# New order of the first steps, and biases through TensorE, in a windowed attention with a softplus feed-forward behind it

## The chip, the cores and the metric

The kernel runs on one core of a Trainium2 chip. A core has five engines with instruction streams of their own: TensorE (PE, matrix products into PSUM), VectorE (DVE), ScalarE (ACT, functions such as exp and ln), GpSimd (POOL) and SyncE (SP). Each works through its own instructions in the order in which the program gives them, and waits on semaphores for the others. In this kernel POOL issues the loads that cast from float32 to bfloat16, and SP issues the transposes by DMA and the stores. The metric is the time of one execution on the device in microseconds (us).

## The reference

Four sequences of 768 tokens, 8 heads of 64; 3072 tokens in all. The attention sees the first 8 tokens of the sequence and the last 96 tokens; each head has a penalty that is linear in the distance. What comes out goes through a feed-forward layer of width 2048 with softplus.

```
scores = (q @ k.T) / 8                               # per batch and head
rel = pos[:, None] - pos[None, :]
keep = (pos[None, :] < 8) | ((rel >= 0) & (rel < 96))
dist = where(is_global & ~is_local, 96, abs(rel))
scores = where(keep, scores - slope[h] * dist, -1e9) # slope[h] = 2 ** -(h + 1)
a = softmax(scores)
x = (a @ v) laid out as (3072, 512)
g = softplus(x @ w_in)                               # w_in 512 x 2048
out = g @ w_out                                      # w_out 2048 x 512
```

## The kernel before, in words

The tokens are cut into 24 blocks of 128, six to a sequence, and the feed-forward works on 12 chunks of 256 tokens, two blocks to a chunk. All steps have short names, and the order in which they stand in the program is the order on every engine.

For block n:

- `lN` loads q and k of block N, `lvN` loads v (L97, on POOL, 128 KB each in bfloat16). Block 0's q and k come in float32 over SP (L84, L85) and are cast on VectorE (`cq0`, `ck0`, L441 and L444).
- `tN` transposes q and k on TensorE against the identity (L203) and VectorE copies the result to QT and KT (L209, L215). `tq` and `tk` do the same for q and k apart. From block 8 on, `dN` does it by DMA from SP (L227, L228).
- `gkN` and `gvN` copy the keys and values of the sequence's first 8 tokens into the block before (L240, L244), so that the window and the global tokens come out of two blocks.
- `sN.h` makes the scores of half h of the heads: 8 products (4 in a sequence's first block) into `s_ps` (L253), and VectorE adds the bias of the distance into Z (L265 or L267). Each half's scores use the one buffer `s_ps`. From block 8 on both halves are made in one step, the second in the banks `tr` and `o2` (L275, L276).
- `eN.h` takes exp of Z on ScalarE into Pb (L289).
- `pN.h` multiplies Pb with v (L302, in `x_ps`), and VectorE divides by the sum (L313, L316).
- `xN` transposes the result into XT, on TensorE for the first six blocks (L331), by DMA from SP after that (L327).

For the feed-forward, chunk c has 8 steps `f` (number 8c + u): each makes 256 of the 2048 columns with 8 products of 256 columns (L347), and ScalarE makes softplus as ln(1 + exp) from it in two passes (L352, L353). The products go to `hT`, which has two buffers. 8 steps `o` (number 8c + u) multiply the result with w_out in 4 products of 512 columns (L367). `wiN` and `woN` load a quarter each of w_in and w_out (L102, L108, 512 KB each in bfloat16). `gN` is a POOL instruction that waits for step fN, and so holds back POOL's later loads (L404).

The bias tables come from a ramp (POOL, L142) and a few VectorE steps (`tables`), and from 24 ScalarE multiplications: `b0`, `b1` (L181), `bb0`, `bb1` (L185). `wN` is a run of N filler products of 512 columns on zeros (L438), which compute nothing that is used.

The order of the first steps is written out by hand as a text (ORDER, L411 to L422), up to f27. All later steps are sorted by due times: `fN` at N + 0.5, `oN` at N + LAG + 0.9 with LAG = 13, attention of block n around 4n - 10.4 (`steady`, L424).

Of the kernel before, what the change touches and what calls it, by code (L numbers as in the profile page):

```python
# [9 lines left out]
AF = mybir.ActivationFunctionType  # L10
# [9 lines left out]
def kernel(  # L20
# [47 lines left out]

# [10 lines left out]
    w_in_c = [const.tile([P, KM, FW], BF16, name=f"w_in{c}") for c in range(NWC)]  # L79
# [5 lines left out]
    nc.sync.dma_start(k_f[:], k[0, :, 0:P, :].rearrange("h s d -> s h d"))  # L85
# [5 lines left out]
    warm_in = const.tile([P, DM], BF16, name="warm_in")  # L91
# [9 lines left out]
    def load_w_in(c):  # L101
        nc.gpsimd.dma_start(  # L102
            w_in_c[c][:],
            moe_w_in[:, c * FW : (c + 1) * FW].rearrange("(m p) f -> p m f", p=P),
        )
# [40 lines left out]
    make_identity(nc, ident)  # L146
    load_qk(1)
    load_v(0)
    load_v(1)
    load_qk(2)  # L150
    load_qk(3)

    def tables():
        nc.vector.tensor_scalar(
            far_a[:], rampf[:], float(NL - 1), FAR, op0=ALU.is_gt, op1=ALU.mult
        )
# [3 lines left out]
        nc.vector.tensor_copy(dist_0[:], dist_d[:])  # L160
        nc.vector.tensor_scalar_min(dist_0[0:NG, :], dist_0[0:NG, :], float(NL))
        nc.vector.tensor_scalar(
            far_b[:], rampf[:], -float(P - NL + 1), FAR, op0=ALU.is_gt, op1=ALU.mult
        )
        nc.vector.scalar_tensor_tensor(dist_p[:], rampf[:], float(P), far_b[:], ALU.add, ALU.add)
        nc.vector.memset(dist_p[0:NG, :], float(NL))

    tables()
    ones(2, RV)

    load_w_in(0)
    load_v(2)
    load_w_in(1)
    load_v(3)

    def head_of(half, r):
        return 4 * half + 2 * ((r // 2) % 2) + r // 4

    def bias_first(half):
        for r in range(0, 8, 2):  # L180
            nc.scalar.mul(bias0[:, half, r // 2, :], dist_0[:], -slopes[head_of(half, r)])  # L181
# [223 lines left out]


    LAG = 13

    ORDER = """  # L411
# [109 lines left out]
```

## Time and profile before

| what | value |
|---|---|
| time, median of 3 runs | 217.99 us (217.25 to 218.74) |
| profiled execution, first to last instruction | 215.9 us |
| what lies around that span, against the median | 2.1 us |
| TensorE busy | 208.5 us (97%) |
| ScalarE busy | 163.4 us (76%) |
| VectorE busy | 115.8 us (54%) |
| POOL busy | 74.1 us (34%) |

The profiled execution gives the span alone; the 2.1 us is the difference to the median of the runs. Busy TensorE counts every product, fillers too, and a product's row lasts until its last result is written, so that rows overlap; the chain of waits gives the distance at which they follow each other. In the chain and in the timeline the first number is the start in us from the first instruction, the second the length in us. In the group rows, "x768 | 98.5, 273" says 768 instructions, 98.5 us busy, 273 ns each. In a timeline row, square brackets hold the idle time ahead of it and what ended it. "DMA to landing" is the time from the start of the issuing instruction until the data is there. A row of stretches gives the stretch, and then the busy time (and number of instructions) of PE, PEld (weight loads), DVE, ACT and POOL, the granted clock, the DMA share and GB/s.

### The profile page before, as it was taken

How to read it: one execution, taken by the hardware profiler on the slowest of the kernel's cores; microseconds unless marked ns; L12 is line 12 of the kernel's file. 1: busy time of each engine (PE TensorE's matmuls, PEld its weight loads, DVE VectorE, ACT ScalarE, POOL GpSimd, SP SyncE). 2: the span in 40 equal slices, each digit the busy share in tenths (PEclk: the TensorE clock that was granted, in tenths of full speed). 3: DMA queues.
4: the chain of work that ended last, by engine and by line, in shares of the span. 5: the costliest groups of instructions: out<-in, count | busy, mean ns of one | idle time of the engine just before them, and what ended most of it. 6: DMA issues, size and time to landing. Idle time of an engine off the chain costs nothing.

```text
span 215.9 us, 5010 instructions
## 1 busy us (share of the span) xinstructions
PE 208.5 (97%) x1986; PEld 140.8 (65%) x1986; DVE 115.8 (54%) x258; ACT 163.4 (76%) x266; POOL 74.1 (34%) x117
## 2 busy tenths in 40 slices
PE   7789999999999999999999999999999999999994
PEld 2356876666768666666676666667667667666553
DVE  5798933687593464464674674364574573011121
ACT  7746999849898979768878878868978978777300
POOL 8995445524253524334334334343311000000000
PEclk9999999999999999999999999999999999999999
DMA  8999999999998999999999999999992620211112
GB/s 125 152 185 183 207 183 198 164 173 145 140 130 102 146 173 147 142 147 104 155 108 128 153 115 127 154 128 110 161 140 47 98 73 8 68 52 49 49 49 97
DMA packets 109927, 27.06 MB, mean 125 GB/s; under 512 B 102608, under 2 KB 106960, under 8 KB 109904
## 3 DMA queue, kind: packets, MB, share of 16 engines
q0 software_dynamic: 77024, 13.37, 83.2%
q1 hardware_dynamic: 32880, 13.38, 31.3%
q8 instruction: 15, 0.25, 0.5%
q14 instruction: 8, 0.07, 0.1%
HBM read 27.26 MB, written 6.29 MB: 155 GB/s over the span
## 4 chain that ended last, share of the span: by engine, by line
PE 86%; ACT 6%; DVE 4%; DMA 2%; issue 1%; SPq 0%; DVEq 0%
PE o L367 38%; PE hT L347 36%; PE x_ps L302 4%; PE s_ps L253 4%; DVE Z L267 2%; ACT G L353 2%; DMA k_f<-in_k_dram 2%; ACT Pb L289 2%; ACT e_sb L352 2%; PE o L389 2%; PE s_lo L253 1%; PE tr L203 1%; DVE Z L265 1%; DVE k_t L444 0%; PE tr L331 0%
## 5 line engine op out<-in xcount | busy, mean ns | idle before, releaser
L347 PE MATMUL hT<-XT,w_in 128*128 128x256 bf16 x768 | 98.5, 273 | 0.1
L367 PE MATMUL o<-w_out,G 128*128 128x512 bf16 x368 | 92.8, 379 | 0.0
L347 PEld LDWEIGHTS <-w_in 128*128 128x128 bf16 x768 | 74.2, 98 | 25.0 <-issue 0.3
L352 ACT ACTIVATE e_sb<-hT 128x512 f32<-128x512 f32 x96 | 56.5, 588 | 21.8 <-PE hT L347 20.8
L353 ACT ACTIVATE G<-e_sb 128x512 bf16<-128x512 f32 x96 | 60.5, 630 | 3.6
L289 ACT ACTIVATE Pb<-Z 128x1024 bf16<-128x1024 f32 (+1 forms) x48 | 46.7, 977 | 11.1 <-DVE Z L267 9.8
L367 PEld LDWEIGHTS <-G 128*128 128x128 bf16 x368 | 32.2, 98 | 26.9
L267 DVE TENSOR_TENSOR Z<-s_ps,biasA 128x1024 f32<-128x1024 f32 x26 | 31.8, 1222 | 12.3 <-PE s_ps L253 12.3
L313 DVE RECIPROCAL rcp<-x_ps 128x4 f32<-128x4 f32 x48 | 8.7, 181 | 45.7 <-PE x_ps L302 45.5
L373 DVE COPY osb<-o 128x512 f32<-128x512 f32 x23 | 15.8, 685 | 26.6 <-PE o L367 26.5
L404 POOL COPY gate_t<-G 1x1 bf16<-1x1 bf16 x32 | 5.7, 178 | 67.4 <-ACT G L353 67.4
L97 POOL DMA_DIRECT2D q_t<-in_q_dram x23 | 20.5, 892 | 10.6 <-issue 5.3
L97 POOL DMA_DIRECT2D v_t<-in_v_dram x24 | 21.3, 886 | 6.4 <-PE x_ps L302 2.4
L97 POOL DMA_DIRECT2D k_t<-in_k_dram x23 | 20.5, 891 | 4.3 <-PE s_ps L253 1.9
L316 DVE TENSOR_TENSOR xsf<-x_ps,rcp 128x256 bf16<-128x256 f32 x48 | 20.4, 424 | 1.7
L302 PE MATMUL x_ps<-v_t,Pb 128*128 128x65 bf16 x352 | 18.6, 193 | 0.1
L302 PEld LDWEIGHTS <-Pb 128*128 128x128 bf16 x352 | 16.7, 98 | 2.8 <-ACT Pb L289 0.8
L253 PEld LDWEIGHTS <-KT 64*128 64x128 bf16 x352 | 10.3, 94 | 8.4 <-issue 7.0
L253 PE MATMUL s_ps<-QT,KT 64*128 64x128 bf16 x232 | 12.1, 218 | 0.9 <-DVE Z L267 0.6
L438 PE MATMUL warm_ps<-warm_in 128*128 128x512 bf16 x26 | 8.9, 445 | 1.2 <-DVE v_t L89 1.2
L284 DVE TENSOR_TENSOR Z<-s_hi,biasA 128x512 f32<-128x512 f32 x14 | 9.5, 681 | 0.0
L284 DVE TENSOR_TENSOR Z<-s_lo,biasA 128x512 f32<-128x512 f32 x14 | 9.5, 681 | 0.0
(49 smaller groups left out, 81.7 us busy)
## 6 DMA issues: line engine op xcount, KB each, us to landing
out_dram<-osb SPq DMA_DIRECT2D x23, 256.0 KB, 3.2
v_t<-in_v_dram POOLq DMA_DIRECT2D x24, 128.0 KB, 4.6
q_t<-in_q_dram POOLq DMA_DIRECT2D x23, 128.0 KB, 4.6
k_t<-in_k_dram POOLq DMA_DIRECT2D x23, 128.0 KB, 5.1
w_in<-in_moe_w_in_dram POOLq DMA_DIRECT2D x4, 512.0 KB, 9.0
w_out<-in_moe_w_out_dram POOLq DMA_DIRECT2D x4, 512.0 KB, 13.5
XT<-xsf SPq DMA_TRANSPOSE x18, 4.2
q_f<-in_q_dram SPq DMA_DIRECT2D x1, 256.0 KB, 3.3
```

Source lines behind the costliest of these rows:

```text
L97: nc.gpsimd.dma_start(dst[n][:, :, 0:D], src[b, :, i * P : (i + 1) * P, :].rearrange("h s d -> s h d"))
L253: nc.tensor.matmul(dst(4 * sub + 2 * mm + t), KT[n - t][rows, m, :], QT[n][rows, m, :])
L267: nc.vector.tensor_tensor(Z[:], s_ps[:], biasA[:, half, :, :], ALU.add)
L284: nc.vector.tensor_tensor(Z[:, regs, :], s_i[:, 0:4:step, :], bias[:, 1, regs, :], ALU.add)
L289: nc.scalar.activation(Pb[:, 0:nreg, :], Zt.pop((n, half))[:, 0:nreg, :], AF.Exp, scale=inv_sqrt)
L302: nc.tensor.matmul(x_ps[:, lh, :], Pb[:, r, :], v_t[n - t][:, h, :], start=(t == 0), stop=(t == 1 or first),)
L316: nc.vector.tensor_tensor(xsf[:, h0 : h0 + 4, :], x_ps[:, :, 0:D], rcp[:, h0 : h0 + 4][:, :, None].to_broadcast([P, 4, D]), ALU.mult,)
L347: nc.tensor.matmul(hT[:, j, :], w_in_c[wc][:, m, fo : fo + P], XT[c][:, m, :], start=(m == 0), stop=(m == KM - 1),)
L352: nc.scalar.activation(e_sb[:], hT[:], AF.Exp)
L353: nc.scalar.activation(G[c][:, 2 * u : 2 * u + 2, :], e_sb[:], AF.Ln, bias=1.0)
L367: nc.tensor.matmul(o[:], G[c][:, 4 * kq + a, ns * P : ns * P + P], w_out_c[kq][:, a, :], start=(kq == 0 and a == 0), stop=(kq == NWC - 1 a ...
L373: nc.vector.tensor_copy(osb[:], O.pop((c, ns))[:])
```

## The change

Four things change together.

1. **Order.** ORDER is written anew and reaches to f36 and o24 (about token 1400). Loads of q and k become steps of their own (`lq`, `lk`) and all loads stand in ORDER: q, k, v of blocks 1 to 3 come ahead of the first quarter of w_in except for v3. The feed-forward begins with f0 f1 f2, then takes chunk 1's f8 to f11 ahead of chunk 0's f3 to f7, and the weights come in that order. LAG becomes 11. The transposes `x` by DMA are called `y`.
2. **Bias by TensorE.** For blocks 0 to 3 a new step `zN.h` writes minus slope times distance into PSUM by 4 products of a scaled identity (`slope_id`) with the distance table (128 columns in block 0, 256 otherwise), and the scores are added onto it in PSUM. ScalarE takes exp from PSUM. VectorE's additions for these blocks go. The two halves have buffers of their own: `s_ps`, and `oo` in the two banks that are `o` and `o2` later.
3. **Tables.** The distance tables become bfloat16, VectorE makes the identity and the 8 scaled identities, and half 1's bias tables (`b1`, `bb1`) are one ScalarE multiplication each of half 0's.
4. **Small things.** k of block 0 is loaded over ScalarE's DMA queue; fillers have 256 columns, are 16 at the start and then one ahead of single steps, and are written into the buffer of the step behind them; `tk0` uses the bank `tr` as `tq0` does; Pb has four buffers; blocks 0 and 1 use `hT` buffers for half 1 of `p` and for `x`.

```diff
-    nc.sync.dma_start(k_f[:], k[0, :, 0:P, :].rearrange("h s d -> s h d"))
+    nc.scalar.dma_start(k_f[:], k[0, :, 0:P, :].rearrange("h s d -> s h d"))
...
-    make_identity(nc, ident)
-    load_qk(1)
-    load_v(0)
-    load_v(1)
-    load_qk(2)
-    load_qk(3)
...
+    nc.vector.tensor_scalar(ident[:], rampf[:], 0.0, 1.0, op0=ALU.is_equal, op1=ALU.mult)
...
+    for h in range(H):
+        nc.vector.tensor_scalar_mul(slope_id[:, h, :], ident[:], -slopes[h])
...
-    load_w_in(0)
-    load_v(2)
-    load_w_in(1)
-    load_v(3)
...
     def bias_rest(half):
+        if half:
+            nc.scalar.mul(biasA[:, 1, :, :], biasA[:, 0, :, :], HALF_RATIO)
+            return
...
+    def fill(dst):
+        for _ in range(fillers[0]):
+            nc.tensor.matmul(dst, warm_in[:, 0:P], warm_in[:, 0 : dst.shape[1]])
+        fillers[0] = 0
...
-    def qk(n, half, dst):
+    def qk(n, half, dst, pre=False):
...
+                        start=not pre,
+                        stop=not pre or (mm == 1 and (t == 1 or n == first_of(n))),
...
+    NPB = 4
+    def early(n, half):
+        return (oo if half else s_ps)[:, :, :]
+    def z(n, half):
+        buf = early(n, half)
+        fill(wide(buf))
+        for j in range(4):
+            sub, mm = divmod(j, 2)
+            h = 4 * half + 2 * mm + sub
+            if n == first_of(n):
+                nc.tensor.matmul(
+                    buf[:, 2 * j, :], slope_id[:, h, :], dist_0[:], start=j % 2 == 0, stop=False
+                )
+            else:
+                nc.tensor.matmul(
+                    buf[:, 2 * j : 2 * j + 2, :], slope_id[:, h, :], dist_dp[:],
+                    start=j % 2 == 0, stop=False,
+                )
...
     def sc(n, half):
+        if n < NPB:
+            fillers[0] = 0
+            buf = early(n, half)
+            qk(n, half, lambda r: buf[:, r, :], pre=True)
+            return
+        fill(wide(s_ps[:]))
...
     def ex(n, half):
         nreg = 4 if n == first_of(n) else 8
-        Pb = work.tile([P, 8, P], BF16, tag="Pb", name="Pb")
...
+        Pb = work4.tile([P, 8, P], BF16, tag="Pb", name="Pb")
+        if n < NPB:
+            src = early(n, half)[:, 0 : 8 : 8 // nreg, :]
...
-    LAG = 13
+    LAG = 11
     ORDER = """
-        w8 b0 bb1 cq0 ck0 tq0 w1 tk0 w2 s0.0 b1 tq1 bb0 tk1 w1 e0.0 s0.1 e0.1
-        l4 wi2 wi3 wo0 l5 lv4 wo1 lv5 wo2 wo3
-        w2 p0.0 s1.0 t2 l6 lv6 p0.1 e1.0 w1 s1.1 gk2 e1.1 w2 x0 p1.0 w2 s2.0 t3 l7 lv7 e2.0 p1.1
-        w2 s2.1 e2.1 gk3 w2 x1 gv2 w3 s3.0
-        f0 p2.0 f1 s3.1 e3.0 p2.1 e3.1 f2 gv3 t4 gk4 f3 p3.0 x2 s4.0 p3.1 f4 f5 s4.1 x3 f6 gk5
...
+        w16 b0 cq0 ck0 z0.0 tq0 z0.1 b1 tk0 s0.0 bb0 lq1 s0.1 e0.0 lk1 lv0 e0.1 t1 lq2 z1.0 lk2 lv1 z1.1
+        p0.0 p0.1 s1.0 s1.1 e1.0 t2 gk2 x0 p1.0 lq3 w1 z2.0 e1.1 w1 s2.0 lv2 lk3 p1.1 z2.1 wi0 s2.1 e2.0
+        e2.1 gk3 gv2 t3 p2.0 w1 z3.0 x1 lv3 s3.0 p2.1 bb1 e3.0 z3.1 s3.1 e3.1 gv3 x2 p3.0 wi2 f0 lq4 lk4
+        p3.1 f1 x3 f2 lk5 f8 t4 lq5 f9 wo0 wi4 f10 gk4 s4.0 t5 f11 lv4 s4.1 lq6 o4 lk6 o0 wi6 e4.0 gk5 lv5
+        e4.1 f3 gv4 f12 wo1 s5.0 f4 p4.0 t6 f13 s5.1 e5.0 f5 p4.1 lq7 lk7 wo2 f14 lv6 gv5 g9 lq8 lk8 s6.0
+        e5.1 p5.0 x4 f15 s6.1 f6 e6.0 o1 t7 p5.1 wo3 f7 s7.0 g13 lv7 d8 x5 e6.1 lk9 w1 o5 o6 g15 o2 f16 lv8
+        f17 p6.0 s7.1 f18 f19 p6.1 lq9 w1 o7 e7.0 e7.1 f20 g17 y6 d9 w1 gk8 o3 f21 p7.0 s8.0 g19 o8 lq10
...
     def tr_first_k(n):
-        tr = ps.tile([P, 2, NPAIR, P], BF16, tag="o2", name="tr_k")
+        tr = qk_bank()
```

More of the change, by code (lines that the diff above doesn't have):

```diff
@@ L296, in pv @@
         Pb = Pt.pop((n, half))
+        x_b = x_ps
+        if n < 2 and half:
+            x_b = ps2.tile([P, 4, D + 1], F32, tag="hT", name="x_b")
+        fill(wide(x_b[:]))
         for lh in range(4):
@@ L355, in o_bank @@
     def o_bank(i):
[L356 removed]
+        return o_tile(i, [P, DM])
     def ffn2(c, u):
@@ L429, in steady @@
             f"e{n}.0": s + 0.7, f"e{n}.1": s + 1.7, f"p{n}.0": s + 1.95, f"p{n}.1": s + 2.95,
[L430 removed]
+            f"y{n}": s + 3.25,
         }
[L433 removed]
+    fillers = [0]
     def warm(count):
[L437 to L438 removed]
+        fillers[0] += count
     def cast_q(n):
```

144 lines of the change are left out of this document (87 added, 57 removed).

## The prediction

> **What bounds the kernel now.** I read the page first, then the stretches, the timeline of TensorE, and last the chain of waits in order of time.
>
> ```profile
> span 215.9 us, 5010 instructions
> PE 208.5 (97%) x1986; PEld 140.8 (65%) x1986; DVE 115.8 (54%) x258; ACT 163.4 (76%) x266; POOL 74.1 (34%) x117
> ...
> PEclk9999999999999999999999999999999999999999
> ...
> PE 86%; ACT 6%; DVE 4%; DMA 2%; issue 1%; SPq 0%; DVEq 0%
> ```
> ```profile
> 10.00:15.00 5.00, 4.13 (x56) 2.55 (x55) 4.93 (x12) 2.34 (x3) 5.00 (x7) 1.00 1.70 175
> 15.00:20.00 5.00, 4.49 (x53) 2.84 (x54) 4.96 (x10) 2.32 (x3) 2.69 (x4) 1.00 1.83 181
> ...
> 100.00:120.00 20.00, 20.00 (x207) 13.74 (x205) 12.22 (x26) 16.23 (x26) 7.02 (x12) 1.00 1.32 119
> ```
> ```profile
> 1.19 3.32 PE L438 MATMUL warm_ps<-warm_in 128*128 128x512 bf16 x8 [1.19 <-DVE v_t L89]
> ...
> 18.72 1.03 PE L347 MATMUL hT<-XT,w_in 128*128 128x256 bf16 x8
> ...
> 47.78 1.91 PE L347 MATMUL hT<-XT,w_in 128*128 128x256 bf16 x16
> ```
>
> The span lies 2.1 us under the median of 217.99; I take these 2.1 us as fixed. TensorE has no gap in the later stretches (20.00 of 20), so there the time is its work. That can't shrink, since every step stays. Between 10 and 20 us VectorE is full instead (4.93 and 4.96 of 5.00), and part of TensorE's busy time there is filler. The first feed-forward step is at 18.72. So a gain can only come from the start: how early TensorE is full of real work.
>
> The chain of waits gives the spacing of each kind of step, and what carries the start:
>
> ```profile
> 1.26 4.37 DMA k_f<-in_k_dram
> ...
> 5.66 0.71 DVE k_t L444
> ...
> 6.42 0.41 PE tr_k L203 x4
> ...
> 6.85 0.44 DVE KT L215
> ...
> 7.74 0.70 DVE Z L265
> ...
> 10.27 1.23 DVE Z L267
> 11.50 0.02 issue
> 11.52 1.07 ACT Pb L289
> ...
> 23.05 1.04 ACT Pb L289
> 24.09 0.49 ACT e_sb L352
> ...
> 24.60 0.63 ACT G L353
> ...
> 31.40 0.45 PE tr L203 x8
> 31.84 0.86 PE o L367 x4
> 32.71 0.87 PE hT L347 x8
> ...
> 34.44 0.33 PE s_ps L253 x8
> ...
> 37.49 0.24 PE x_ps L302 x8
> ...
> 41.02 0.22 PE tr L331 x4
> ```
>
> From 7.7 to 18.7 the chain is a ring over one buffer: scores, VectorE's addition (0.70 or 1.23), exp (1.07). Now I count **lost time**: the clock minus real TensorE work at these spacings. At 47.78, where f16 begins, done are t0 to t7 (8 x 0.45 = 3.6), scores of blocks 0 to 6 (10 halves x 0.33, and 4 half-sized ones of 0.2: 4.1), p up to p6.0 (10 x 0.24 and 3 x 0.13: 2.8), x0 to x5 (6 x 0.22 = 1.3), 16 f (13.9) and 8 o (6.9): 32.6 us. Lost: 15.2.
>
> **The change, part by part.** *Bias by TensorE.* VectorE loses 2 x 0.70 and 6 x 1.23 = 8.8 us, all of it in the ring. TensorE gains 8 z steps: two of 4 x 128 columns, six of 4 x 256. A z of 1024 columns is half of an f (2048 columns, 0.87): 0.43; together 6 x 0.43 + 2 x 0.22 = 3.0 us. They stand where the fillers stood: 26 fillers of 512 columns become 18 of 256 (16 at the start, one each ahead of z2.0 and z3.0; the others are set to nothing by the step behind them). With that cover gone z would cost its 3.0 us in full. A z waits until exp has read its buffer, and on TensorE behind it stand t, x and p steps; but with two buffers one half's z and scores run beside the other's exp. exp reads PSUM where it read SBUF; the nearest rows are the two passes of a step f, of which the one out of PSUM is not slower (0.49 against 0.63), so nothing; the other end is the difference, 0.14 for each of 8.
>
> *Tables.* The 8 scaled identities are VectorE steps of a kind that the trace lacks:
>
> ```profile
> L154 DVE TENSOR_SCALAR far_a<-rampf 128x128 f32<-128x128 f32 x1 | 0.2, 227 | 0.0
> L160 DVE COPY dist<-dist_d 128x128 f32<-128x128 f32 x1 | 0.5, 457 | 0.0
> L89 DVE MEMSET v_t<- 128x8 bf16 x8 | 0.3, 65 | 0.0
> L185 ACT ACTIVATE biasA<-dist_d 128x128 f32<-128x128 f32 x8 | 2.3, 292 | 0.0
> ```
>
> Between 65 ns and 457 ns each, 0.5 to 3.7 us; I take 0.15, the distance at which L154 and its like follow each other (nearest in kind and size): 1.2 us. The tables ended at 3.8; with the identity they end near 4.9. The cast of q began at 4.07, so it comes 0.8 later, which is hidden, as k lands only at 1.26 + 4.37 = 5.63. At 3.7 us the chain would start 2 us later. On ScalarE, 12 multiplications and two wide ones (bounded by 0.49 and 1.07) replace 24; they end by 6, before the first exp. `bb1` stands ahead of e3.0 and takes 1.0 us there.
>
> *First scores.* k over ScalarE's queue: issuing costs ScalarE about 0.5 ahead of its table load, hidden. Landing between 4.04 (where q landed) and 5.63; I take 5.4. Then 0.71 (cast), 0.44 (copy of QT, now ahead, since `tk0` waits for the bank `tr`), 0.41, 0.44: first scores at 7.45, against 7.33. The Trainium skill, "DMA: Bandwidth & Descriptors", section "Issuing engines are not separate DMA queues", says that another issuing engine saves only the time of issuing. By that k would land at 5.6 and the scores come at 7.65; no run here shows k on ScalarE's queue yet. The next stage absorbs such differences, as follows.
>
> *Blocks 0 to 3.* Exp of a half takes 0.95 to 1.07; e0 at 7.8 to 8.9, s1 at 9.7, e1 to 12.05, e2.1 to 14.4, `bb1`, e3.0 15.4 to 16.4, p3.0, x2, and f0 at 16.85. ScalarE is the ring's limit now, VectorE is not: its copies (0.44 each) fit between.
>
> *Loads.* POOL's issues and landings:
>
> ```profile
> 1.29 0.33 POOL masks.py:199 TENSOR_SCALAR_AFFINE_SELECT ident<-ident 128x128 bf16<-128x128 bf16 x1
> 1.57 1.02 POOL L97 DMA_DIRECT2D q_t<-in_q_dram  x1
> ...
> 7.80 0.93 POOL L97 DMA_DIRECT2D k_t<-in_k_dram  x1
> 8.67 0.81 POOL L102 DMA_DIRECT2D w_in<-in_moe_w_in_dram  x1
> ...
> 13.65 1.60 POOL L102 DMA_DIRECT2D w_in<-in_moe_w_in_dram  x2
> ...
> 30.14 0.89 POOL L97 DMA_DIRECT2D q_t<-in_q_dram  x1 [2.98 <-DMA q_t<-in_q_dram]
> ```
> ```profile
> DMA to landing us min/median/max: 4.6/4.6/4.6
> ```
> ```profile
> DMA to landing us min/median/max: 6.2/6.2/6.2
> ```
> ```profile
> DMA to landing us min/median/max: 9.9/10.8/11.7
> ```
>
> These answers are for k3 (issued 7.80), the first quarter of w_in (8.67) and the next two late ones (13.65, 14.4). They land at 12.4, 14.87, 23.55 and 26.1: 2.5 us per quarter once the queue is full. Between them the q, k, v take 0.85 to 0.9 each, as they are issued. Without the identity POOL starts 0.5 sooner, but v2 now stands ahead too: k3 lands at 12.8, `wi0` at 15.3, `wi2` 18.7, k4 20.4, `wo0` 24.7, `wi4` 27.2, k6 29.9, `wi6` 32.4, `wo1` 35.8, k7 37.6, `wo2` 40.1, `wo3` 45.3.
>
> *From f0 to f16.* I follow the new order, each step at the latest of three: TensorE free, its data landed, its `hT` given back by the exp of the f two before. A step f costs ScalarE 1.14 (0.49 + 0.63 and the way), an exp 0.95 to 1.04. f2 comes at 19.1 (behind wi2), t4 20.85, o4 25.1, f12 27.75, t6 30.05, f14 32.85, o1 36.55, t7 37.7, o6 40.85, f16 at 42.55. ScalarE is full meanwhile (16 f and ten exps to 40.8), and loads land 0.1 to 1.2 us before their step, or make it wait by 0.1; TensorE still loses only about 1 us. A start that is 0.4 us earlier gives the same f16. By then done are the t's (3.6), scores with s7.0 (4.4), p0 to p5 (2.7), x (1.3), 16 f (13.9), 6 o (5.2): 31.1. Lost: 11.45, z and fillers in it. Against 15.2 that is a gain of 3.7 us. The stall on VectorE's additions goes; what is late next is ScalarE and the weight loads, together.
>
> *Behind f16* block 8's transposes go out on SP ahead of the first store where they stood behind it; I count nothing, since 7 us lie between k8's landing (42.8 at the rate above) and s8.0, near 50. TensorE is full as before; LAG 11 moves o steps by two f steps, which neither adds nor removes any. **Sum: 217.99 - 3.7 = 214.3.**
>
> **The rivals.** *The loads give part back.* The order asks for each weight as it lands. For: the landings above are within 1.2 us of their use, and block 8's transposes by DMA now go out while weights still load. Against: the rate is one the trace shows. At 3.0 instead of 2.5 us per quarter, the sixth, `wo2`, comes 3 us late and TensorE idles about 2.5: 216.8. The same result stands for a change that does not do what it says, the VectorE stall being only exchanged for ScalarE's: 40.8 us of ScalarE work 6% longer costs 2.4.
>
> *The clock drops: slower than before.* The 8 first fillers took 3.32 us, 0.415 each, where an o product of the same 512 columns takes 0.86 / 4 = 0.215. TensorE ran at half speed until about 4.5 and at full speed behind; the granted clock, 9 throughout, doesn't show that. In the new kernel, fillers end at 4.5 and until the second block's scores near 9.7 TensorE has only z0, z1, t0, t1, s0, p0, about 2.5 us of work in 5. If that lets the half speed come back and stay until f0, the 9.4 us of work up to there (6.2 real, 3.0 z, two fillers) take 18.8: f0 at 4.6 + 18.8 = 23.4 in place of 16.85, and 214.3 + 6.6 = 220.9. It decides at a busy share under that of before, where fillers kept it near 3.6 of 5. The Trainium skill, "TensorE: Matmul & The Clock Gate", Part 1, says that the clock goes to half after an idle window of about 3.4 us and back after a busy one. By that rule the trace's first 3.32 us agree, and the new kernel's gaps, under 1 us each, would not trip it; no run here shows how busy is enough.
>
> *More gain.* If ScalarE reads PSUM faster and the loads come sooner, f16 could come 1.5 us earlier: 212.8.
>
> **How the numbers follow.** Forecast 214.3, within 213.4 to 215.8: 0.58. Loads or ScalarE give back part, 215.8 to 218.5: 0.24. Clock, or stalls that add up to as much, above 218.5: 0.11. More gain, under 213.4: 0.07. The range 212.8 to 218 leaves out 0.03 below and 0.15 above. One per cent, about what a measurement here can tell from no change, is 215.8 and 220.2: faster 0.63, same 0.26, slower 0.11.
>
> **What would show it.** Right: no VectorE addition before s4.0; exp on `s_ps` and `oo` back to back from about 8; f0 near 17, f16 near 42.5, TensorE without gaps behind, span near 212.2. Wrong: waits of TensorE on w_in, w_out or k between 18 and 46 (loads); z products spaced at 0.21 instead of 0.11 after 5 us (clock); first scores behind 8.5 (tables); a gap at s8.0 (transposes of block 8).

## The result, and the profile after

The changed kernel takes 216.53 us (median of 10 runs, 215.40 to 217.78) where the kernel before, run beside it, takes 218.17 us (10 runs): the ratio is 0.9923 with a 95% interval of 0.9899 to 0.9947. The gain is 1.64 us of the 3.7 that were forecast: less than one per cent, on the right side of zero, and inside the range of 212.8 to 218. The profiled execution has a span of 215.5 us and took 217.24 us, above the median. Execution against execution the two profiles therefore differ by less, 215.5 against 215.9 us of span; the profile before is of the quickest of its ten executions (217.25). A few executions of the experiments f0_ahead, extra_load and k_by_SP were over 1.5% slower than the fastest of the same kernel, and their medians below leave these out, as all ratios do.

Engines and the shares of the chain, from the page of the changed kernel:

```profile
span 215.5 us, 5039 instructions
PE 207.6 (96%) x2010; PEld 143.5 (67%) x2010; DVE 109.8 (51%) x260; ACT 162.0 (75%) x255; POOL 73.9 (34%) x115
...
PE 85%; DMA 6%; POOL 4%; issue 1%; DVE 1%; ACT 0%; SPq 0%; POOLq 0%; DVEq 0%
```

VectorE's and ScalarE's shares of the chain (4% and 6%) are down to 1% and 0%. In their place stand DMA, from 2% to 6%, and POOL with 4%, which issues the loads. The stretches show the same at the start:

```profile
10.00:15.00 5.00, 4.50 (x74) 3.32 (x73) 4.16 (x14) 4.38 (x5) 5.00 (x7) 1.00 1.73 153
15.00:20.00 5.00, 3.76 (x64) 2.99 (x62) 2.94 (x10) 2.51 (x4) 3.14 (x4) 1.00 1.64 186
```

Between 15 and 20 us VectorE has 2.94 us of work where it had 4.96. But TensorE is busy for only 3.76 us, less than before (4.49, fillers in it), and ScalarE is half idle (2.51 of 5). So none of these three holds the end of blocks 0 to 3. What does is in the chain of waits in order of time, and in TensorE's timeline:

```profile
9.80 0.74 POOL w_in L105
10.54 7.97 DMA v_t<-in_v_dram
18.51 0.04 issue
18.55 0.40 PE x_ps L363 x8
18.95 0.87 PE hT L416 x8
...
54.70 5.78 DMA KT<-k_t
...
60.53 0.42 PE s_ps L277 x8
```
```profile
7.08 0.29 PE L277 MATMUL s_ps<-QT,KT 64*128 64x128 bf16 x4 [0.52 <-DVE KT L241]
...
14.08 0.40 PE L229 MATMUL tr<-ident,k_t 128*128 128x128 bf16 x4 [0.49 <-DMA k_t<-in_k_dram]
...
18.55 0.40 PE L363 MATMUL x_ps<-v_t,Pb 128*128 128x65 bf16 x8 [1.19 <-DMA v_t<-in_v_dram]
18.79 1.04 PE L416 MATMUL hT<-XT,w_in 128*128 128x256 bf16 x8
...
21.02 1.91 PE L416 MATMUL hT<-XT,w_in 128*128 128x256 bf16 x16
...
44.55 1.91 PE L416 MATMUL hT<-XT,w_in 128*128 128x256 bf16 x16
...
60.53 0.40 PE L277 MATMUL s_ps<-QT,KT 64*128 64x128 bf16 x8 [0.71 <-DMA KT<-k_t]
...
64.56 1.05 PE L416 MATMUL hT<-XT,w_in 128*128 128x256 bf16 x8 [0.47 <-ACT Pb L348]
```

First scores come at 7.08, f0 at 18.79, f2 at 21.02, f16 at 44.55. The waits say which data was late. t3 waits 0.49 us for k of block 3. p3.0, the step ahead of f0, waits 1.19 us for v of block 3, which stands in the queue behind the first quarter of w_in and lands 7.97 us after it is issued, at 18.51. Without these 1.68 us f0 would be near 17.1. That the second quarter lands at 20.9, just ahead of f2, follows from its issue and its landing time; the answers for the first quarter (issued 9.80), v3 (10.54) and the second quarter (11.41):

```profile
DMA to landing us min/median/max: 7.7/7.7/7.7
```
```profile
DMA to landing us min/median/max: 8.0/8.0/8.0
```
```profile
DMA to landing us min/median/max: 9.5/9.5/9.5
```

The prediction's own measure fits what came out. Up to f16 there are 31.1 us of real work, so the time lost is 44.55 - 31.1 = 13.45 us, against 15.2 before: a gain of 1.75, and 1.64 were measured between the medians. That the two lie so close is in part luck. This execution lost some of the gain again behind f16: from f16 to the last group of products it takes 164.10 us, and 162.98 in the second profile of the same kernel, whose span is 214.5.

### The profile page after: what moved, and what is told of

It is laid out like the page before. It is cut to its first block, busy times and chain, and to the rows that moved or that the text cites. A ratio compares the mean times of both kernels' runs of the same rounds, so it can differ in the third digit from the quotient of the medians.

```text
span 215.5 us, 5039 instructions
## 1 busy us (share of the span) xinstructions
PE 207.6 (96%) x2010; PEld 143.5 (67%) x2010; DVE 109.8 (51%) x260; ACT 162.0 (75%) x255; POOL 73.9 (34%) x115
## 4 chain that ended last, share of the span: by engine, by line
PE 85%; DMA 6%; POOL 4%; issue 1%; DVE 1%; ACT 0%; SPq 0%; POOLq 0%; DVEq 0%
PE hT L416 38%; PE o L438 35%; PE x_ps L363 4%; DMA v_t<-in_v_dram 4%; PE s_ps L277 4%; DMA KT<-k_t 3%; PE o L460 2%; POOL v_t L99 1%; PE s_lo L277 1%; POOL q_t L99 1%; POOL k_t L99 1%; PE tr L229 1%; DVE Z L339 1%; ACT Pb L348 0%; PE tr L396 0%
## 5 line engine op out<-in xcount | busy, mean ns | idle before, releaser
L438 PE MATMUL o<-w_out,G 128*128 128x512 bf16 x368 | 91.8, 379 | 0.0
L421 ACT ACTIVATE e_sb<-hT 128x512 f32<-128x512 f32 x96 | 56.5, 589 | 25.7 <-PE hT L416 24.8
L438 PEld LDWEIGHTS <-G 128*128 128x128 bf16 x368 | 32.8, 98 | 27.9
L348 ACT ACTIVATE Pb<-Z 128x1024 bf16<-128x1024 f32 (+1 forms) x40 | 39.0, 982 | 6.3 <-DVE Z L316 6.1
L316 DVE TENSOR_TENSOR Z<-s_ps,biasA 128x1024 f32<-128x1024 f32 x20 | 24.4, 1222 | 18.8 <-PE s_ps L277 14.6
L377 DVE TENSOR_TENSOR xsf<-x_ps,rcp 128x256 bf16<-128x256 f32 x46 | 19.5, 424 | 1.6
L363 PE MATMUL x_ps<-v_t,Pb 128*128 128x65 bf16 x340 | 17.9, 193 | 1.2 <-DMA v_t<-in_v_dram 1.2
L277 PE MATMUL s_ps<-QT,KT 64*128 64x128 bf16 x204 | 10.6, 219 | 1.2 <-DMA KT<-k_t 0.7
L339 DVE TENSOR_TENSOR Z<-o,biasA 128x512 f32<-128x512 f32 x14 | 9.5, 679 | 0.0
L268 DVE COPY v_t<-v_t 8x512 bf16<-8x512 bf16 x16 | 7.5, 468 | 0.0
## 6 DMA issues: line engine op xcount, KB each, us to landing
w_in<-in_moe_w_in_dram POOLq DMA_DIRECT2D x4, 512.0 KB, 10.5
```

Source lines behind the costliest of these rows:

```text
L277: nc.tensor.matmul(dst(4 * sub + 2 * mm + t), KT[n - t][rows, m, :], QT[n][rows, m, :], start=not pre, stop=not pre or (mm == 1 and (t == ...
L316: nc.vector.tensor_tensor(Z[:], s_ps[:], biasA[:, half, :, :], ALU.add)
L339: nc.vector.tensor_tensor(Z[:, regs, :], s_i[:, 0:4:step, :], bias[:, 1, regs, :], ALU.add)
L348: nc.scalar.activation(Pb[:, 0:nreg, :], src, AF.Exp, scale=inv_sqrt)
L363: nc.tensor.matmul(x_b[:, lh, :], Pb[:, r, :], v_t[n - t][:, h, :], start=(t == 0), stop=(t == 1 or first),)
L377: nc.vector.tensor_tensor(xsf[:, h0 : h0 + 4, :], x_b[:, :, 0:D], rcp[:, h0 : h0 + 4][:, :, None].to_broadcast([P, 4, D]), ALU.mult,)
```

## The experiments

Two theories run through the expectations. The **loads theory**: v of block 3 and the quarters of w_in come later than forecast and pace the start. Its rival: **TensorE and ScalarE pace it** anyway, and the loads only lie beside. Beside them stand single causes: the clock, LAG, the transposes behind f16. The starts of f0, f2 and f16 are from each run's profile, which is one execution; the ratios are to the kernel before on the same chip.

**The same kernel again.** No edit.

> The changed kernel as it is, beside the kernel before on the same chip, as the measure for the three that follow. Every theory: 216.5 us, a ratio near 0.992, f0 at 18.8 and f16 at 44.5 us of its span, with p3.0 waiting about 1.2 us for v of block 3 and s9.0 about 0.7 us for the transpose of block 9's keys.

216.51 us, ratio 0.9924 (0.9898 to 0.9950); f0 at 18.87, f2 21.10, f16 44.72, span 214.5. The result stands. In this execution TensorE ran at half speed until about 10.5 us (z1.0, the bias of block 1's half 0, takes 1.06 us where the first profile has 0.60), so the chain of blocks 0 to 3 was itself late, and v of block 3 was waited for by 0.32 us only. Two delays lie beside each other here, and the later one counts.

**f0 ahead of p3.0**, so that nothing ahead of f0 asks for v of block 3.

```diff
-gv3 x2 p3.0 wi2 f0 lq4 lk4  p3.1 f1 x3 f2
+gv3 x2 wi2 f0 lq4 lk4  f1 p3.0 p3.1 x3 f2
```

> f0 and f1 move ahead of p3.0, so that they need only the first quarter of w_in (landed at 17.5 us in the changed kernel) and no longer stand behind the wait for v of block 3 (landed at 18.5). Theory L (the load queue paces everything up to f16): f0 starts at 17.5, but f2 still waits for the second quarter at 20.9 and all later steps for their loads, so f16 stays at 44.5 within 0.3 us and the time within 0.4 us of the changed kernel. Theory S (ScalarE is full from f0 on, and f0's start alone sets the rest): f16 comes 1.1 to 1.3 us earlier and the time is 1.2 us less, about 215.3.

217.32 us, ratio 0.9981 (0.9954 to 1.0008): no gain is left that can be measured. TensorE's timeline of this run:

```profile
18.05 1.92 PE L416 MATMUL hT<-XT,w_in 128*128 128x256 bf16 x16 [0.79 <-DMA w_in<-in_moe_w_in_dram]
...
20.95 0.40 PE L363 MATMUL x_ps<-v_t,Pb 128*128 128x65 bf16 x8 [0.73 <-DVE xsf L377]
...
22.09 0.28 PE L396 MATMUL tr<-ident,xsf 128*128 128x128 bf16 x2 [0.62 <-DVE xsf L377]
22.21 1.91 PE L416 MATMUL hT<-XT,w_in 128*128 128x256 bf16 x16
```

f0 is 0.74 us earlier and now waits for w_in itself. But f0 and f1 stood between p3.0, p3.1 and x3 and covered VectorE's divisions; without that cover TensorE waits 0.73 and 0.62 us, f2 comes 1.2 us later, and f16 at 45.68.

**f0 alone ahead of p3.0.**

```diff
-gv3 x2 p3.0 wi2 f0 lq4 lk4  p3.1 f1 x3 f2
+gv3 x2 wi2 f0 lq4 lk4  p3.0 f1 p3.1 x3 f2
```

> f0 alone moves ahead of p3.0, without the mistake of the earlier try, which put f1 ahead too and so left the three ends of block 3 (p3.0, p3.1, x3) without cover. f0 needs the first quarter of w_in (17.5); p3.0 follows at 18.5 when v of block 3 has landed. Theory L: f2 still waits for the second quarter at 20.9, f16 at 44.4, no gain beyond 0.3 us. Theory S: ScalarE begins 1.1 us earlier, f16 0.8 to 1.1 us earlier, the time 215.5.

217.01 us, ratio 0.9950 (0.9924 to 0.9975); f0 18.11, f2 21.38, f16 45.34. x3 waits 0.62 us for VectorE. In this execution the clock fell as well (granted 0.50 from 8 to 10 us), x2 came at 17.87 instead of 16.97, and f0 stands right behind it. So the profile doesn't show what f0 would do at full speed; the time is no better than that of the changed kernel with its wait for v.

**One more load ahead of w_in**: v of block 3 is loaded a second time, 128 KB, into a tile that nothing reads.

```diff
+        if u == 0:
+            nc.gpsimd.dma_start(v_x[:], v[0, :, 3 * P : 4 * P, :].rearrange("h s d -> s h d"))
         nc.gpsimd.dma_start(w_in_c[u][:], ...)
```

> One more load of 128 KB (v of block 3 into a tile that nobody reads) is put on POOL's queue ahead of the first quarter of w_in; nothing else changes. Theory L: every load behind it lands about 0.9 us later, f0 at 19.7 and f16 at 45.4, the time about 0.9 us more (217.4). Theory S: f0 is later by 0.9 as well, since p3.0 waits for a load, but ScalarE's later gaps take part of it back; f16 0.3 to 0.6 us later. A theory by which loads do not matter: no change.

217.82 us, ratio 0.9986 (0.9955 to 1.0016). f0 19.38, f2 21.61, f16 45.08: 0.59, 0.59 and 0.53 us later than in the changed kernel; t3 waits 1.00 us for k3 and p3.0 1.35 us for v3. The steps follow the queue. The time rose by more, 1.3 us. The profile's span is 1.6 us longer than the changed kernel's, and all of that lies behind the last group of products, which starts at 208.63 (208.65 in the changed kernel); so the time settles nothing here, the steps do.

**Two loads left out.** v of blocks 2 and 3 isn't loaded; VectorE fills the tiles with ones. The output of blocks 2 to 4 is another one.

```diff
-lq3 w1 z2.0 e1.1 w1 s2.0 lv2 lk3      x1 lv3 s3.0
+lq3 w1 z2.0 e1.1 w1 s2.0 lk3          x1 s3.0
-nc.vector.memset(v_t[n][:, :, D : D + 1], 1.0)
+e0 = 0 if n in (2, 3) else D
+nc.vector.memset(v_t[n][:, :, e0 : D + 1], 1.0)
```

> The loads of v of blocks 2 and 3 are left out; their tiles are set to ones by VectorE at the start instead, so that all steps still run, with other values for blocks 2 to 4. POOL's queue is two small loads shorter. Theory L (the landings set f0 and the steps up to f16): the first quarter of w_in lands at 15.5 to 16, the rest 1.7 to 2 us earlier each; p3.0 waits for nothing, f0 at 17.2 to 17.4, f16 at 42.7 to 43.0, the time 214.7 to 215.1, and the prediction's way from f0 to f16 (25.7 us) is confirmed with only its landings wrong. Theory S (ScalarE paces from f0 on): f16 comes by as much earlier as f0 does, 1.4 to 1.6 us, and the way stays at 25.7; the two agree here. A theory by which f0 was late for another reason: no change.

217.34 us, ratio 0.9963 (0.9940 to 0.9987). It doesn't tell the theories apart: filling the tiles took VectorE 1.08 us ahead of the first cast, TensorE waited 1.41 us for its first operand, first scores came at 8.30, the clock fell again (granted 0.50 from 10 to 12 us), and the chain of blocks 0 to 3 ended at 19.1 by itself.

**v of block 3 in front of w_in.**

```diff
-p1.1 z2.1 wi0 s2.1      x1 lv3 s3.0
+p1.1 z2.1 lv3 wi0 s2.1  x1 s3.0
```

> v of block 3 goes ahead of the first quarter of w_in on POOL's queue. Both theories: v3 lands at about 15.0 and p3.0 runs at 17.2 without a wait, but the weights land at 18.4 and hold f0 there, 0.4 us earlier than before at best; f16 and the time within 0.4 us of the changed kernel. If the time falls by 1 us, it was v3 and not the queue as a whole.

217.25 us, ratio 0.9942 (0.9913 to 0.9972). The timeline of TensorE:

```profile
16.91 0.41 PE L363 MATMUL x_ps<-v_t,Pb 128*128 128x65 bf16 x8
18.85 1.05 PE L416 MATMUL hT<-XT,w_in 128*128 128x256 bf16 x8 [1.53 <-DMA w_in<-in_moe_w_in_dram]
```

The wait only changes its name. p3.0 is done at 17.15, so the chain of blocks 0 to 3 without waits for v is 0.3 us behind the forecast of 16.85; f0 waits for w_in until 18.8 all the same.

**A first quarter of half the size**, the other half behind v of block 3.

```diff
-W_IN = {0: 2, 2: 2, 4: 2, 6: 2}
+W_IN = {0: 1, 1: 1, 2: 2, 4: 2, 6: 2}
-x2 p3.0 wi2 f0
+x2 p3.0 wi1 wi2 f0
```

> The first quarter of w_in is loaded in two halves, the second one behind v of block 3, so that f0 needs 256 KB instead of 512 KB and v of block 3 stands behind 256 KB less. Theory L: v3 lands at 17.3, f0 at 17.5, f1 at 18.7 behind the second half; the quarter behind that lands at 20.9 to 21.3 as before, so f2 and f16 (44.5) stay and the time is that of the changed kernel within 0.4 us. Theory S: f16 0.8 to 1.1 us earlier, 215.5.

216.53 us, ratio 0.9920 (0.9887 to 0.9953): as the changed kernel. f0 comes at 17.80, 1.0 us earlier, f2 at 20.68, 0.34 earlier, f16 at 44.41, 0.14 earlier. The queue has the same bytes ahead of f2. An early f0 alone is worth nothing.

**The first quarter over SP's queue**, in float32, cast by ScalarE in four pieces.

```diff
+nc.sync.dma_start(w0_f[:], moe_w_in[:, 0 : 2 * CT].rearrange("(m p) f -> p m f", p=P))
+def cast_w(j): nc.scalar.copy(w_in_c[0][:, :, cols], w0_f[:, :, cols])
```

> The first quarter of w_in leaves POOL's queue: SP loads it in float32 right at the start, and ScalarE casts it in four pieces of 128 x 512 (0.55 us each, two behind e0.1, one behind e2.1, one ahead of e3.0). Everything behind it on POOL's queue is one weight load sooner. Theory L (the landing of v of block 3 and of the weights sets f0 and the pace up to f16): v3 lands 2.5 to 3 us earlier, p3.0 is free at about 17.2, f0 at 17.3 in place of 18.8, f16 at 43, the time 215.0 to 215.4. If the sixteen DMA engines and not POOL's queue set the pace, the 1 MB more at the start delays q and k of block 1 by 2 us and nothing is gained (216.5 or more). Theory S (ScalarE sets the pace): its 2.2 us of casts cost at least 1 us, 217 or more.

219.04 us, ratio 1.0020 (0.9995 to 1.0046); f0 21.74, f16 47.73. The timeline of TensorE:

```profile
9.05 0.61 PE L231 MATMUL tr<-ident,q_t 128*128 128x128 bf16 x4 [1.52 <-DMA q_t<-in_q_dram]
```

q of block 1, alone at the head of POOL's queue, now lands after 7.7 us instead of 4.8, since it shares the DMA engines with 1 MB of weights. The Trainium skill, "DMA: Bandwidth & Descriptors", section "Issuing engines are not separate DMA queues", says that loads share the DMA engines whichever engine starts them; the trace agrees. Behind the wait TensorE runs at half speed (granted 0.50 from 10 to 12 us, z1.0 1.06 us), which adds to the delay of f0.

**Bias by VectorE in the new order.** No z, no scaled identities; the additions in blocks 0 to 3 are as before, through the one buffer, and `bb1` stands earlier.

```diff
-NPB = 4
+NPB = 0
-z0.0 ... z3.1   (all z steps of the order)
```

> The bias of blocks 0 to 3 goes back to VectorE's additions (one score buffer, no z steps, no scaled identities, half 1's bias table built early); order, loads and tables stay. If the bias by TensorE is worth what the prediction put on it (the ring over one buffer costs 0.70 to 1.23 us per half), p3.0 comes at 20.5 to 21 instead of 18.5, f16 2 us later, and the time is 218 to 218.5, that of the kernel before. If the loads alone set the start (v of block 3 at 18.5), the additions are hidden behind them for the most part and the time is within 0.7 us of the changed kernel.

225.46 us, ratio 1.0326 (1.0297 to 1.0355); f0 25.54, f2 29.81, f16 53.61. The new order without its z steps, around which it was written, is far slower than the kernel before. The stretches and the timeline of TensorE:

```profile
15.00:20.00 5.00, 3.12 (x46) 2.11 (x45) 4.92 (x14) 2.31 (x3) 2.92 (x4) 0.97 1.71 186
20.00:25.00 5.00, 3.39 (x40) 2.42 (x40) 4.64 (x11) 1.94 (x3) 3.42 (x5) 0.50 1.77 182
25.00:30.00 5.00, 4.81 (x37) 3.82 (x37) 1.68 (x6) 2.64 (x4) 1.82 (x3) 0.51 1.79 182
```
```profile
25.54 1.90 PE L413 MATMUL hT<-XT,w_in 128*128 128x256 bf16 x8
```

VectorE is full again (4.92 of 5). And at a busy share of 3.1 to 3.4 in 5, with no wait over 1.59 us, TensorE's clock falls to 0.50 for some 10 us; f0's 8 products take 1.90 instead of 1.04 us.

**The same with fillers**: 28 fillers of 256 columns, ahead of the p steps, which compute nothing that is used.

```diff
-t1 lq2 lk2 lv1  p0.0
+t1 lq2 lk2 lv1  w4 p0.0      (and so at five more p steps)
```

> As the run without z (225.5 us; f0 at 25.5, products of f0 to f2 at half speed, granted clock 0.50 from 20 to 30 us), with 28 more filler products of 256 columns ahead of p steps, about as many columns as the z steps had. They compute nothing. If the loss of 9 us is the additions on VectorE alone, it stays at 225 to 226. If it is the clock that falls when TensorE has too little to do, the products run at full speed, f0 comes at 21 to 22 and the time is 218.5 to 219.5. Both: in between, f0 at 23 to 24 and 221 to 223.

223.88 us, ratio 1.0277 (1.0228 to 1.0326); f0 25.23, f2 27.47, f16 51.23. The clock stays at full speed:

```profile
25.23 1.04 PE L413 MATMUL hT<-XT,w_in 128*128 128x256 bf16 x8
...
51.23 1.91 PE L413 MATMUL hT<-XT,w_in 128*128 128x256 bf16 x16
```

So at least 1.6 us of the loss was the clock (the fillers' own work, up to 28 x 0.11 = 3.1 us, isn't taken off), and most of the rest is the ring over VectorE: f0 comes at 25.23 against 18.79. This run tells something else too. The weights had long landed when they were asked for (the third quarter, `wo0`, at 26.6 with f2 at 27.47; in the changed kernel 27.1 and 21.02), and still f16 comes 26.0 us behind f0 and 23.8 behind f2. In every run of the new order f2 to f16 takes 23.4 to 24.0 us, however late f2 is. From f2 on the loads don't pace it: TensorE and ScalarE do, as the prediction had it (23.45). The loads bind ahead of that, at f0 and f2.

**LAG as it was before.**

```diff
-LAG = 11
+LAG = 13
```

> LAG back to 13 in the changed kernel. Prediction's step: the lag adds and removes no work and TensorE has no gap behind f36, so the time is that of the changed kernel within 0.4 us (216.1 to 216.9). If the shorter lag makes products wait for the softplus, or shortens the end, it shows as a difference of 0.8 us or more.

216.64 us, ratio 0.9920 (0.9895 to 0.9945): no difference. This run's profile caught the clock rival at work, in TensorE's timeline and in the stretches:

```profile
5.31 0.40 PE L229 MATMUL tr<-ident,q_t 128*128 128x128 bf16 x4 [0.65 <-DVE q_t L510]
...
6.51 0.38 PE L229 MATMUL tr<-ident,k_t 128*128 128x128 bf16 x4 [0.58 <-DVE QT L235]
...
8.73 1.06 PE L301 MATMUL s_ps<-dist_dp,slope_id 128*128 128x256 bf16 x4
```
```profile
6.00:8.00 2.00, 0.97 (x14) 0.69 (x15) 0.88 (x3) 0.20 (x1) 2.00 (x3) 0.88 2.07 132
8.00:10.00 2.00, 2.00 (x14) 1.64 (x15) 0.76 (x2) 0.89 (x2) 2.00 (x3) 0.50 2.10 134
10.00:12.00 2.00, 2.00 (x36) 1.68 (x34) 1.03 (x4) 0.56 (x1) 2.00 (x4) 0.77 2.31 147
```

At 5.3 us the transposes take 0.40, full speed. Then TensorE is busy for 0.97 of 2 us, and from about 7.5 to 10.5 the clock is 0.50; z1.0 takes 1.06 instead of 0.60. No wait in between is over 0.65 us. x2 comes at 18.03 instead of 16.97. f0 comes at 19.59 and f16 at 45.30, 0.8 us later than in the changed kernel, because v of block 3 is late again: POOL's issue of k of block 1 took 1.78 us instead of 0.88.

**q of block 9 loaded earlier**, right behind k of block 9, so that SP's transposes go out sooner.

```diff
-e6.1 lk9 w1 o5      p6.1 lq9 w1 o7
+e6.1 lk9 lq9 w1 o5  p6.1 w1 o7
```

> The load of block 9's q moves ahead of the gate on f15 and of v of block 8 on POOL's queue; nothing else changes. In the changed kernel that q landed at 53.4, its transposes by DMA went out on SP at 53.5 and 54.7, and s9.0 waited 0.7 us for the keys and f24 0.5 us for XT of block 7, whose transpose stands behind them on SP. If this queue is what took part of the gain back behind f16, q of block 9 lands about 1 us earlier, both waits go, and the time is 0.3 to 1.2 us less than the changed kernel's (215.4 to 216.2). If not, no change.

216.79 us, ratio 0.9945 (0.9918 to 0.9972), span 214.0. The waits of 0.71 us at s9.0 and 0.47 at f24 are gone from its profile, but the time isn't less by what can be measured. The same kernel again had 0.2 and none of the two, so they belong to the one profiled execution more than to the median.

**The old order of the loads** (v1 behind v0; v2 behind the first quarter, v3 behind the second), to see whether the order makes the first quarter slow.

```diff
-lk1 lv0 ... lk2 lv1 ... lv2 lk3 ... wi0 ... lv3 s3.0 ... wi2
+lk1 lv0 lv1 ... lk2 ... lk3 ... wi0 lv2 ... wi2 lv3 s3.0
```

> The order of the loads is that of the kernel before (q1 k1 v0 v1 q2 k2 q3 k3 wi0 v2 wi2 v3), the steps stand as in the changed kernel. Theory A (the first quarter takes 7.7 us from issue to landing because of what is loaded ahead of it): 6.2 us as before, issued near 8.9, landed near 15.1; v2 then lands near 16, the second quarter near 18.7, v3 near 19.5. p2.0 would wait for v2 by about 2 us and p3.0 for v3, so f0 comes near 20.3 and f2 near 22.5: no gain, ratio 0.995 to 1.003. Theory B (the landing time has another cause than the order): still 7.3 to 7.8 us, landed near 16.5, f0 later still, near 21.5, ratio 0.998 to 1.008.

221.65 us, ratio 1.0135 (1.0089 to 1.0181): p2.0 waits 4.57 us for v2, f0 23.45, f16 49.53. The first quarter takes 7.2 us to land with the same loads ahead of it as in the kernel before, where it took 6.2. The order isn't the cause.

**k of block 0 over SP again.**

```diff
-nc.scalar.dma_start(k_f[:], ...)
+nc.sync.dma_start(k_f[:], ...)
```

> k of block 0 is loaded over SP's queue again, behind q. Theory A (which queue issues makes only the difference of issuing): k lands 0.4 to 0.6 us later, first scores at 7.5 to 7.7 in place of 7.08; v of block 3 still sets f0, so f0 stays at 18.8, f2 at 21.0 and the ratio at 0.990 to 0.994. Theory B (the order in which q and k go out changes what the load queue gets): the first quarter of w_in lands in another time than 7.3 to 7.8 us, near 6.2, and f2 comes 1 us or more earlier.

217.71 us, ratio 0.9947 (0.9914 to 0.9980); first scores 7.08, f0 18.41, f2 20.64, f16 44.31; the first quarter lands after 7.4 us. So that isn't the cause either, and k over ScalarE's queue brings the first scores nothing. The time lies above the changed kernel's with an earlier f16. In the profile that is the very end: the last group of products starts 0.9 us earlier (207.76 against 208.65), but SP's last two stores take 3.37 us instead of 1.52. Why they do, and whether the median has the same cause, stays open.

**Two loads left out, without work for VectorE**: p of blocks 2 to 4 reads v of block 1 where it read blocks 2 and 3; their output is another one.

```diff
-lq3 w1 z2.0 e1.1 w1 s2.0 lv2 lk3      x1 lv3 s3.0
+lq3 w1 z2.0 e1.1 w1 s2.0 lk3          x1 s3.0
-v_t[n - t][:, h, :]
+v_t[1 if n - t in (2, 3) else n - t][:, h, :]
```

> The loads of v of blocks 2 and 3 are left out, and the p steps of blocks 2 to 4 read v of block 1 in their place (their output differs on purpose); nothing else changes, and VectorE gets no work for it, unlike in two_less. Theory A (the 2 us between forecast and result are the later landings of the load queue): the queue is 1.75 us shorter, so the first quarter of w_in lands near 16 and the second near 19; f0 begins at 16.9 to 17.3, f2 at 19.2 to 19.6, f16 23.5 to 24.0 behind f2, at 42.8 to 43.5, and the time is 1.2 to 1.8 us under that of the changed kernel (ratio to before 0.984 to 0.987). Theory B (TensorE and ScalarE pace the start, the loads only lie beside): f2 stays within 0.5 us of 21.0 and the ratio is 0.990 to 0.994.

216.42 us, ratio 0.9889 (0.9831 to 0.9948), four runs far apart (215.5 to 217.57). The profile shows no wait for a load at the start, but z1.0 at 1.06 us, half speed until 10.5: f0 18.49, f2 20.80, f16 44.27. With the loads out of the way the clock was the later delay. The same kernel follows once more, and then one with four fillers meant to hold the clock up:

> two_less_b once more, word for word the same kernel (v of blocks 2 and 3 not loaded, that of block 1 read in its place). Its profile had the z products of block 1 at half speed (1.06 us for 4 of 256 columns) until about 10.5 us, so that the chain of blocks 0 to 3 itself gave f0 at 18.49. If the products run at full speed (0.60) from 8 us on in this profile: f0 at 17.0 to 17.6, f2 at 19.3 to 19.8, f16 at 42.8 to 43.6 (theory: late loads and half speed are two delays beside one another, and taking both away gives the forecast). If f16 stays at 44.2 to 44.6 though f0 is at 17.3, something else holds f2 to f16. At half speed again: f0 18.4 to 18.8, f16 44.1 to 44.6.

```diff
-tq0 z0.1 b1 tk0      e0.1 t1 lq2 z1.0
+tq0 w2 z0.1 b1 tk0   e0.1 t1 lq2 w2 z1.0
```

> two_less_b with two fillers more ahead of z0.1 and two ahead of z1.0 (they compute nothing that is used; v of blocks 2 and 3 not loaded). Theory clock (half speed comes from a thin share of work between 5 and 8 us): full speed is there from 8 us on in the profile, f0 at 17.2 to 17.8, f16 at 43.0 to 43.8, time 1 us or more under the changed kernel's, ratio 0.984 to 0.989. Theory chance (the length of half speed varies whatever the work): no difference to two_less_b beyond the four fillers' own 0.2 to 0.5 us.

215.31 us, ratio 0.9866 (0.9838 to 0.9894), without the fillers, and 215.16 us, 0.9865 (0.9836 to 0.9893), with them. Both profiles have z1.0 at 0.60, so it isn't shown that the fillers hold anything up. TensorE's timeline without the fillers:

```profile
17.02 0.41 PE L363 MATMUL x_ps<-v_t,Pb 128*128 128x65 bf16 x8
17.27 1.04 PE L416 MATMUL hT<-XT,w_in 128*128 128x256 bf16 x8
...
19.73 1.92 PE L416 MATMUL hT<-XT,w_in 128*128 128x256 bf16 x16
...
43.21 1.91 PE L416 MATMUL hT<-XT,w_in 128*128 128x256 bf16 x16
```

f0, f2 and f16 come 1.5, 1.3 and 1.3 us earlier than in the changed kernel, and the time falls by 1.2: that is the loads theory's price, seen from the side where the loads are out of the way. (With 256 KB less to load, later loads come sooner too, so the 1.2 us is an upper end. All eight executions of this one kernel, two_less_b and two_less_c, have a median of 215.60 us, 0.9 less than the changed kernel.) f2 still begins as the second quarter lands, issued at 9.7 and there 10.0 us later, at 19.7.

**The fillers alone.**

> The changed kernel with the same four fillers more. Loads bind f0 (v of block 3) at 18.5 to 18.8 whatever the clock does, so f0, f2 (21.0) and f16 (44.5) stay within 0.3 us and the ratio at 0.990 to 0.994. If instead the time is 0.5 us or more lower, half speed and not the loads sets the median.

216.39 us, ratio 0.9901 (0.9865 to 0.9938); z1.0 at 0.60, and yet p3.0 waits 1.37 us for v3: f0 19.27, f2 21.50, f16 45.26. No difference in time. The first profile of the changed kernel had 0.60 without these fillers, so the better test of the clock is the changed kernel's own two profiles: f0 at 18.79 with z1.0 at 0.60, and at 18.87 with 1.06. With the loads late, full speed earlier buys nothing.

No version here is faster than the changed kernel by what can be measured, other than those that leave loads out.

## Why the prediction was right or wrong

**What bounds it: right.** The gain comes from the start; TensorE is full of work from f0 to f16 (25.76 of 25.76 us), and the time lost up to f16 gives the gain between the medians to 0.1 us, with the luck named above.

**Bias by TensorE: right in kind.** VectorE has no addition in blocks 0 to 3 and the exp out of PSUM takes 1.02 us (1.06 before). Without z the new order, which was written around it, takes 7.4 us more (no_z_fill), or 8.9 with the clock's fall (no_z).

**Tables and first scores: right.** The scaled identities took 1.19 us for 8 (forecast 1.2); k landed at 0.74 + 4.4 = 5.1 (5.4), first scores at 7.08 (7.45).

**Blocks 0 to 3: nearly right.** f0 would have come at 17.1 to 17.3 (v3_first, two_less_c) where 16.85 was forecast.

**Loads: the step that failed.** The prediction had `wi0` landing at 15.3 and `wi2` at 18.7, by taking the landings of the kernel before and moving them by POOL's issues, 0.85 to 0.9 for each q, k or v. They landed at 17.5 and 20.9, 2.2 us later, and v of block 3, between them, at 18.5. So f0 came 1.9 us later than forecast (18.79 against 16.85) and f16 2.0 (44.55 against 42.55), which is what is missing from the 3.7 us. The place of v of block 3 behind 512 KB of weights and the wait of p3.0 for it weren't looked at, although p3.0 stands ahead of f0. Of the 2.2 us, 0.75 is issuing. The first load goes out at 1.34 (1.05 was reckoned), and two issues take longer, 1.21 and 1.06 us. The first of them lies beside VectorE's scaled identities, the second beside its casts of block 0's q and k (4.54 to 5.7). POOL's timeline, and VectorE's row of the identities:

```profile
2.35 0.88 POOL L99 DMA_DIRECT2D k_t<-in_k_dram  x1
3.22 1.21 POOL L99 DMA_DIRECT2D v_t<-in_v_dram  x1
4.42 1.06 POOL L99 DMA_DIRECT2D q_t<-in_q_dram  x1
5.47 0.88 POOL L99 DMA_DIRECT2D k_t<-in_k_dram  x1
```
```profile
2.62 1.19 DVE L159 TENSOR_SCALAR slope_id<-ident 128x128 bf16<-128x128 bf16 x8
```

In no_z, without the identities, the same load of v took 0.88; beside its casts one issue took 1.09 there too, so only the first 0.33 us goes with the identities. The other 1.5 us is the landing time of the first quarter, 7.7 us against the 6.2 before that the prediction carried over. It is 7.2 to 8.2 us in all 17 profiles of the new order in which the whole quarter goes over POOL's queue behind the small loads; the 6.2 stands in one execution. The last two columns of the stretches (DMA share, GB/s) show the queue at the time; first the changed kernel, then the kernel before, then k_by_SP:

```profile
11.00:12.00 1.00, 1.00 (x21) 0.72 (x18) 0.97 (x5) 0.71 (x1) 1.00 (x2) 1.00 2.31 160
12.00:13.00 1.00, 1.00 (x24) 0.70 (x20) 0.69 (x3) 0.75 (x1) 1.00 (x2) 1.00 1.63 124
13.00:14.00 1.00, 0.59 (x12) 0.31 (x8) 0.98 (x3) 0.92 (x2) 1.00 (x3) 1.00 1.17 143
```
```profile
11.00:12.00 1.00, 0.78 (x14) 0.44 (x11) 1.00 (x3) 0.48 (x1) 1.00 (x3) 1.00 1.55 164
12.00:13.00 1.00, 0.83 (x10) 0.44 (x9) 0.97 (x4) 0.58 (x1) 1.00 (x3) 1.00 1.25 199
13.00:14.00 1.00, 0.83 (x16) 0.43 (x15) 1.00 (x3) 0.14 (x1) 1.00 (x2) 1.00 1.28 190
```
```profile
12.00:13.00 1.00, 1.00 (x24) 0.68 (x20) 0.68 (x3) 0.74 (x1) 1.00 (x2) 1.00 1.84 182
13.00:14.00 1.00, 0.60 (x12) 0.32 (x8) 0.98 (x3) 0.91 (x2) 1.00 (x3) 1.00 1.33 182
```

In the changed kernel the last small loads land there (v of block 2 at 12.7, k of block 3 at 14.0), and the queue moves 124 and 143 GB/s for two us. Before, the weights were under way by then, with 199 and 190. But this dip isn't the whole cause: k_by_SP has 182 and 182, and its first quarter still takes 7.4 us. The sums of the stretches show another part. When the first quarter landed, 2.57 MB had been moved in the changed kernel, of which the loads up to that quarter, q and k of block 0 with them, are 2.23 MB; before it was 2.23 of 2.10. So about 0.2 MB more of what stands behind the quarter in the queue had moved beside it, which, as an estimate at the prediction's 2.5 us for 512 KB, is 1.0 us. Why stays open: the order of the loads (old_loads, 7.2), k's queue (k_by_SP, 7.4) and VectorE's scaled identities (no_z, 7.3) aren't it.

**From f0 to f16: right.** 25.76 us measured, 25.7 forecast; f2 to f16 23.53 against 23.45. ScalarE is nearly full there as forecast (23.03 of 25.76 us), with 16 f and six exps, not ten. The landings of the later weights, 2.4 us late (`wo0` 27.1 against 24.7, `wi6` 34.8 against 32.4), cost nothing more, since the steps that use them moved by as much.

**Behind f16: wrong by up to 1.2 us in one execution.** Block 8's transposes were looked at, block 9's weren't: s9.0 waited 0.71 us for the transposed k of block 9, which landed after 5.78 us, and f24 0.47. In the same kernel's other profile the only such wait is 0.23, at s8.0. LAG cost nothing, as said.

**The rivals.** "The loads give part back", 216.8, at 0.24, is what happened, at f0 and f2 and not at the sixth quarter where the prediction put it. "The clock drops" was real in kind and small in size: a fall for about 3 us (lag13), 1.1 us at x2, hidden behind v of block 3; not the 6.6 that it would have cost until f0. Its share of work was set too low: 4.23 of 5 us are busy from 5 to 10 us in the first profile, where 2.5 was forecast. By the rule of the Trainium skill that the prediction named ("TensorE: Matmul & The Clock Gate", Part 1) gaps well under its idle window of about 3.4 us shouldn't trip it. lag13 differs, 0.65 us at most, and so does no_z, whose longest gap was 1.59 us: the measurement decides. That the share of work counts is shown by no_z and no_z_fill; which share is enough isn't.

## What to carry to other kernels

When loads change places in one queue, follow each step back to the last load that it asks for, the small one behind the big one too, and don't carry landing times over from another order: 2 us of this forecast's 3.7 hung on one that was only moved. Before a delay is removed, look for the one that lies beside it. With the loads late, f0 came at 18.79 at full speed and 18.87 at half speed; with two loads left out, at 18.49 at half speed, and only with both delays away at 17.27. And an earlier first product is worth nothing if the second must wait: split_w0 won 1.0 us at f0 and 0.14 at f16.

## What the hardware showed that was not expected

- TensorE's half speed at the start lasts until 4.4 us in some executions, 5.5 to 6.7 in others, and 10.5 in others, of kernels whose first 7 us hold the same instructions. The granted clock in the rows doesn't always show it (1.00 in the same kernel's second profile, where z1.0 took 1.06 us), but showed the fall in lag13 (0.50).
- The clock fell without any long gap: at 0.97 of 2 us busy in lag13, and behind 5 us with 3.12 busy in no_z. Behind the one long wait, 4.57 us in old_loads, it read 0.51 and 0.50 from 19 to 21 us.
- POOL's issue of a load took 1.21 us instead of 0.88 while VectorE wrote eight bf16 tables of 128 x 128 in 1.19 us. In lag13, two_less_b and w0_by_SP the tables took 0.89 us and the issue beside them 1.78: now the one, now the other is held up.
- The first 512 KB load behind the small ones took 7.2 to 8.2 us to land in 17 profiles of the new order and 6.2 in the one of the kernel before, with no cause found.
- SP's last two stores took 1.52 us in the changed kernel and 3.37 in k_by_SP: a profile's span can be 1.8 us longer by its last steps alone.
